# Last two attention units normalised on TensorE, a split out-projection, and new planner constants in a two-layer transformer kernel

## Chip, cores and metric

The kernel runs on one core of a Trainium2 chip. Its time is device microseconds of one execution; the median of three runs of the kernel before is 1628.04 us (1627.45 to 1629.54).

## What is computed

Two identical layers over 2048 rows of width 512. Each layer is an attention block and a gated feed-forward block, with the residual kept:

```python
x = x + _A_ref(_layernorm(x, axis=-1), A_wqkv, A_wo)               # 32 heads of width 16, softmax, out-projection
x = x + _B_ref(_layernorm(x, axis=-1), B_w_gate, B_w_up, B_w_down) # (gelu(x Wg) * (x Wu)) Wd, hidden width 1792
```

and both lines once more. In `_A_ref` the scores are q k^T / 4, the softmax runs over all 2048 keys, and each head's output is the softmax row times v. Inputs are bf16.

## The kernel before

The instruction order is not written by hand. A planner in `_emit_fast` runs at build time: it keeps a modelled clock for each engine, and at every step of its main loop it picks what TensorE does next, records it, and lets VectorE, GpSimd and SyncE take the jobs that have become ready ("pump", L490). Engines then run their recorded streams in order, with semaphore waits. So every constant of the planner moves instructions on all engines.

**Units.** Queries are cut into 4 blocks of 512 rows, heads into 8 groups of 4. A unit is one block and one group. Scores come out transposed (128 keys by 512 queries) in 64 tiles per unit: L1395, four heads side by side in the rows of the array. A tile is exponentiated either by ScalarE, two or three tiles in one ACTIVATE (L1409, written to fPT), or by VectorE, which makes the bits of an fp16 power of two (L1449, fPI) and three shifted copies (L1489, fPP). P times V (L1541) then accumulates in PSUM bank 7 with four heads in the columns of the array; a column of ones in V gives each head's row sum. In the last layer the last block is split in two halves of 256 queries, F0 and F1, 8 units each, so that F0's feed-forward can lie beside F1's attention.

**Closing a unit** (`evac` L936, `normalise` L863). VectorE copies bank 7 to fOS (L947). The row sums lie along one partition per head; a DMA turns them (fLT), VectorE inverts them (L871) and checks their bounds (L879), a DMA writes them to DRAM (rscr), the unnormalised heads go to DRAM too (oscr, four transfers), and for each pair of units two DMAs bring back the heads packed (fOP) and the inverse sums spread over partitions (fRB). GpSimd multiplies them into fAT (L912). Units are gathered in groups `sizes`: 6 and 2, and for F1 6, 1 and 1. The DMAs of F1's last unit are issued from ScalarE's queue (`move_act`), all others from SyncE's.

**After a block** (`post` L1042): out-projection (`mm_piece`, its matmuls at L643) plus residual (L1058), layer-norm statistics (L587, L588), scale on GpSimd (`ln_scale` L590: add of epsilon L595, power L597), application (L610), transposes (L616, or by DMA), gate (L1073, copied at L1092), Gelu (`gelus` L1353, which needs a table load on ScalarE and one back to Exp; for F1, L1095 applies Gelu to the gate's bank directly), up (L1073, multiplied at L1116), down (L1137), and the residual (L1159 or L1168). These are the "pieces" that the planner fits between the tiles of the next block.

**What sets the order.** `fill_ready` (L1314) gives the time F at which the next score tiles could start. P-times-V groups and pieces go in only if they end by then, or by the end of ScalarE's current work, plus a tolerance: 0.1 us for projections, 1.0 us for a `post` that is behind its pace, 99 us once it is behind by more than `LAG` = 24 us (`post_tol` L1659). `DVE_LATE` (L201) caps VectorE's backlog when it takes a tile. When nothing fits, and TensorE's modelled share of work in the last 3.4 us is under `DENSE` = 0.7, `keep_clock` (L1555) issues four matmuls on zeros, recorded at L1561.

Of the kernel before, what the change touches and what calls it, by code (L numbers as in the profile page):

```python
# [175 lines left out]
def _emit_fast(nc, es, x_in, wqkv, wo, wg, wu, wd, out, n_rep=2):  # L176
# [23 lines left out]
    NPART = 6  # L200
    DVE_LATE = 2.82  # L201
    WAIT_D = 0.45
# [37 lines left out]
    OS = sb("fOS", [128, NOS, 512], F32)  # L240
    LT = sb("fLT", [128, 128], F32)
    NRB = 1
    RB = sb("fRB", [128, NRB, 512], F32)
# [30 lines left out]
    def dma(eng, grp, dst, src, r=(), w=(), serial=False, kb=32):  # L274
        if grp not in sch.groups:
            sch.add_dma_group(grp, serial=serial)
        t = max(sch.free[eng], sch.ready(eng, r, w)) + 0.5
        wire[0] = max(t, wire[0]) + kb / 180.0
        return sch.op(eng, lambda e: e.dma_start(dst, src), r=r, w=w, grp=grp, cost=0.5, lat=wire[0] - t + 1.3)
# [198 lines left out]

    def move_act(prio, grp, dst, src, r, w, then, kb=32):

        then(dma("act", grp + "a", dst, src, r=r, w=w, serial=True, kb=kb))

    def starts_of(eng):
# [95 lines left out]

    def xn(i, alt):  # L580
        return HT[:, i + 4 * alt, 0:D].bitcast(F16)

    def xnkey(i, alt):
        return ("HT", i + 4 * alt)

    def stats(i, rows, key, then=None, prio=1):
        dve(prio, [(lambda e: e.bn_stats(ST[:, i, :], rows), [key], [("ST", i)], 0.72),  # L587
                   (lambda e: e.bn_aggr(MV[:, i, :], ST[:, i, :]), [("ST", i)], [("MV", i)], 0.1)], then)  # L588

    def ln_scale(n, then, lo=0, on="dve"):  # L590
        keys = [("MV", lo + i) for i in range(n)]
        mean = AP(MV, 2 * lo, [[16, 128], [2, n]])
        var = AP(MV, 2 * lo + 1, [[16, 128], [2, n]])
        job("pool", 1, [
            (lambda e: e.tensor_scalar(LNS[:, 0, lo:lo + n], var, LN_EPS, None, op0=ALU.add), keys,  # L595
             [("LNS", lo + i) for i in range(n)], 0.25),
            (lambda e: e.tensor_tensor(LNS[:, 1, lo:lo + n], LNS[:, 0, lo:lo + n], CM05[:, 0:n], op=ALU.pow),  # L597
             [("LNS", lo + i) for i in range(n)] + [("CM05",)], [("LNS", lo + i) for i in range(n)], 0.45 + 0.16 * n),
            (lambda e: e.tensor_scalar(LNS[:, 2, lo:lo + n], mean, -1.0, None, op0=ALU.mult),
             keys + [("LNS", lo + i) for i in range(n)], [("LNS", lo + i) for i in range(n)], 0.25)][:3 if on == "pool" else 2], then)  # L600

# [261 lines left out]
    def normalise(layer, qb, gs, half, h):  # L863
# [7 lines left out]
        ops = [(lambda e: e.reciprocal(LT[:, 0:nw], LT[:, 0:nw]), lk, lk, 0.07 + 0.0068 * nw)]  # L871
        final = h == 1 and gs[-1] == NG - 1
        go = move_act if final else move

        def then(o):
            there = []
            checks = []
            for lim, op in ((1.0 / L_LO, ALU.is_le), (1.0 / L_HI, ALU.is_ge)):
                checks.append((lambda e, lim=lim, op=op: e.scalar_tensor_tensor(  # L879
                    OKL[:, 0:nw], LT[:, 0:nw], lim, OKL[:, 0:nw], op0=op, op1=ALU.mult),  # L880
                    lk + [("OKL",)], [("OKL",)], 0.08 + 0.0018 * nw))
            dve(1, checks, got(("ok", layer, qb, h, gs[-1])))

            def stored(o, i):
                there.append(i)
                if len(there) == n:
                    lt["held"] = False
                    while lt["next"]:
                        lt["next"].pop(0)()
                g = gs[i]  # L890
                rs_here.add((layer, qb, h, g))
                if (layer, qb, h, g ^ 1) in rs_here:
                    pairs_q.append(((layer, qb * NG + (g | 1), h), lambda: spread(g & ~1)))
                    next_pair()

            for i in range(n):
                g = gs[i]
                go(0, "rs%d" % i, AP(RSC, (RC(qb, h, g) * 8 + g % 2) * 512, [[2 * 512, 4], [1, qn]]),
                   LT[:, w * i:w * i + w], [("LT", i)], [("RSC", RC(qb, h, g), g % 2)],
                   lambda o, i=i: stored(o, i), kb=8)  # L900

        def spread(g):
# [14 lines left out]
            def done(o):  # L917
# [6 lines left out]
                 [("OSD", d, j) for d in ds for j in range(4)], [("OP", slot)], landed, kb=qn / 2)  # L924
            go(0, "rb%d" % slot, RB[:, slot, 0:qn],
               AP(RSC, RC(qb, h, g) * 8 * 512, [[512, 8], [0, 16], [1, qn]]),
               [("RSC", RC(qb, h, g), k) for k in range(2)], [("RB", slot)], landed, kb=qn / 2)

# [7 lines left out]
    def evac(layer, u, part):  # L936
# [13 lines left out]
        def then(o):  # L950
# [3 lines left out]
            og = list(range(NG))  # L954
            sizes = [NG - 2, 1, 1] if h == 1 else [NG - 2, 2]
            pos = g
# [7 lines left out]
            bd = block_done[layer, qb, h] = block_done.get((layer, qb, h), 0) + 1  # L964

            gone = []

            def put(o):
                gone.append(o)
                if len(gone) == 4:  # L970
                    os_free.append(s)
                    stored_os.add((layer, u, h))
                    next_pair()
                    if h != 1 or g != NG - 1:
                        gathered(o)

            def put_out(o):
                for j in range(4):
                    move(0, "os%d_%d" % (s, j), OSD[d // 2, 32 * j + 16 * (d % 2):32 * j + 16 * (d % 2) + 16, 0:qn],
                         OS[32 * j:32 * j + 16, s, 0:qn], [("OS", s)], [("OSD", d, j)], put, kb=qn / 16)  # L980
                if h == 1 and g == NG - 1:
                    gathered(o)

# [8 lines left out]
            def gather():  # L992
                (move_act if h == 1 and g == NG - 1 else move)(0, "lt%d" % i, LT[:, w * i:w * i + w],
                     AP(OS, 16 * NOS * 512 + s * 512, [[32 * NOS * 512, 4], [1, qn]]),
                     [("OS", s)], [("LT", i)], put_out)
            if lt["held"]:
                lt["next"].append(gather)
            else:
                gather()
            if bd == NG:  # L1000
                posts.append(post(layer, qb, h))

        dve(0, [(fn, r, [("OS", s)], 0.086 + 0.001042 * qn)], then)

    def wchunk(s, jj, ck):
        return wslot(s)[:, ck * 256 + jj * 128:ck * 256 + (jj + 1) * 128]

    def ln_thread(tts, xsl, check, name, eng, step=2):

        nt = len(tts)  # L1010
        by_dma = step != 1

        def applied(i):
# [6 lines left out]
        def scale(lo):  # L1020
            hi = min(lo + step, nt)

            def apply(o):
                for i in range(lo, hi):
                    ln_apply(i, X[:, xsl[i], :], ("X", xsl[i]), eng, False, applied(i))
            ln_scale(hi - lo, apply, lo, eng)
            if check:
# [3 lines left out]
        for i, tt in enumerate(tts):  # L1031
# [5 lines left out]
            if not by_dma:  # L1037
                yield transpose_piece(i, tt, eng="act" if step == 1 and i % 2 == 0 else "dve", then=got(("tr", name, i)))
        while not all(("tr", name, i) in have for i in range(len(tts))):
            yield None  # L1040

    def post(layer, qb, h):  # L1042
# [10 lines left out]
        xload(n_)  # L1053
        while not all(("norm", layer, qb, h, g) in have for g in range(NG)) or n_ not in xhere:
            yield None
        for i, tt in enumerate(tts):
            def evac_x(b, i=i, x=xsl[i]):
# [5 lines left out]
                           + [("WO",)], evac_x, cols=D)  # L1063
        yield from ln_thread(tts, xsl, True, (layer, qb, 2, h), "dve" if qb == NQB - 1 else "pool",
                             1 if h == 1 else 2)
        xs = slice(512 * qb + q0, 512 * qb + q0 + qn)
# [162 lines left out]
    tiles_filled = [0]  # L1229
    LAG = 24  # L1230
    PRE = 1
# [110 lines left out]
    def fill():  # L1342
# [4 lines left out]
        if d is not None and not k_here(d):  # L1347
            d = None
        for x in a + ([d] if d is not None else []):
            cur.remove(x)  # L1350
# [295 lines left out]
    def behind():  # L1646
# [6 lines left out]
        elif NQB > 1 and posts_done[0] == total_posts - 2:  # L1653
            f = 0.5 * (at + 0.5 * NG - 1.0) / (0.5 * NG - 2.2)
        else:
# [3 lines left out]
    def post_tol():  # L1659
        if pace["haste"] or behind() > LAG:  # L1660
            return 99.0
        return 1.0 if behind() > 0 else 0.1

    sources = [Source(heads(), lambda: 0.1), Source(prep_source(), lambda: 0.1), Source(post_source(), post_tol)]
    DENSE = 0.7
    log = {"idle": 0.0, "warm": 0}

    while True:
# [10 lines left out]
        if posts_done[0] == total_posts and not any(jobs.values()):  # L1679
            break  # L1680
        if gelu_q and sch.ready("act", [("HT", i) for i in range(NFT)]) <= max(t, sch.free["act"]):
            gelus(*gelu_q.pop(0))
# [6 lines left out]
        if F is not None:  # L1689
            limit = max(F, sch.free["act"] - 0.437) - t  # L1690
        its = pv_ready(t)
        byj = [sum(1 for it in its if it[1] == j) for j in range(4)]
        fit = int((limit - change("col")) / MM + 0.29)
        full = min(byj)
# [7 lines left out]
        if press and its:  # L1702
            full = max(full, 1)
        want = 1 if pend.get(("PI", dg["n"] % NPI)) and not dg["items"] else 3
        if fit >= 1 and (full >= want or full and (rest or press)):
# [887 lines left out]
```

## Time and profile before

| | |
|---|---|
| median of three runs | 1628.04 us |
| the profiled execution's own time | 1627.3 us |
| its span | 1625.6 us |
| instructions | 38751 |
| TensorE / VectorE / ScalarE / GpSimd busy | 1546.1 / 1393.4 / 1542.8 / 175.6 us |
| Exp ACTIVATEs (L1409) | 1279: 638 of three tiles, 640 of two, 1 of one |
| tiles on VectorE (L1449) | 901 |
| matmuls of `keep_clock` (L1561) | 1692, busy 141.4 us |
| first exponential starts | 14.7 us |
| Gelu table loads and Gelus on ScalarE before the tail | 7 visits of 1.28 + 6.27 + 1.28 us, 1 of 1.28 + 3.29 + 1.28 us |

Times in views are microseconds from the start of the span. A line number is that of the kernel's source; many operations share the line of a helper. In the groups, the count behind "x" is followed by busy time, the mean of one in ns, and the engine's idle time just ahead of them with what ended it.

### The profile page before, as it was taken

What the parts mean: (1) busy time and instruction counts of PE and PEld (TensorE: products, weight loads), DVE (VectorE), ACT (ScalarE), POOL (GpSimd) and SP (SyncE); (2) the same over time, 40 slices, a digit from 0 to 9 for tenths busy, and PEclk for the clock granted to TensorE, in tenths of its full rate; (3) what the DMA queues carried; (4) which work ended last, traced back from release to release, by engine and by line L of the source; (5) the groups of instructions that cost most, each with busy time, mean ns of one, the idle gap of its engine ahead of it and who ended that gap; (6) DMA issues with size and microseconds to landing.
All of it is one profiled execution on the core that took longest, in us unless ns stands there. A gap on an engine that the chain in (4) does not pass through costs nothing.

```text
span 1625.6 us, 38751 instructions
## 1 busy us (share of the span) xinstructions
PE 1546.1 (95%) x16400; PEld 509.6 (31%) x16400; DVE 1393.4 (86%) x2403; ACT 1542.8 (95%) x1323; POOL 175.6 (11%) x219
## 2 busy tenths in 40 slices
PE   8999999999999999999999999999999999999998
PEld 3333222222222222322332322222222222444454
DVE  7999998889988899987743999988899889898793
ACT  6999999999999999999999999999999999999991
POOL 2321010002100111002410100100110000100000
PEclk9999999999999999999999999999999999999999
DMA  5200111125111421114223111221411114113244
GB/s 149 60 8 6 47 35 53 44 63 123 28 49 47 116 60 34 41 56 109 60 73 111 38 45 34 66 56 31 129 28 43 53 27 123 37 47 88 75 112 134
DMA packets 162370, 103.26 MB, mean 64 GB/s; under 512 B 54928, under 2 KB 145296, under 8 KB 162192
## 3 DMA queue, kind: packets, MB, share of 16 engines
q1 hardware_dynamic: 158096, 95.98, 22.4%
q0 software_dynamic: 2112, 4.19, 1.0%
q8 instruction: 133, 2.18, 0.6%
q10 hardware_dynamic: 1984, 0.53, 0.1%
q14 instruction: 45, 0.37, 0.1%
HBM read 76.81 MB, written 15.20 MB: 57 GB/s over the span
## 4 chain that ended last, share of the span: by engine, by line
PE 42%; ACT 34%; DVE 18%; DMA 3%; issue 1%; POOL 1%; SPq 0%; DVEq 0%; POOLq 0%; ACTq 0%
ACT fPT L1409 32%; PE fPS L1541 12%; PE fPS L1395 12%; PE fPS L1073 9%; DVE fPI L1449 8%; DVE fPP L1489 6%; PE fPS L1137 4%; PE fPS L643 3%; ACT fHT L1358 2%; DMA fRB<-rscr 2%; PE fPS L1561 1%; DMA rscr<-fLT 1%; DVE fQ L689 1%; DVE fHT L1092 1%; DVE fOS L947 1%
## 5 line engine op out<-in xcount | busy, mean ns | idle before, releaser
L1409 ACT ACTIVATE fPT<-fPS 128x1536 bf16<-128x1536 f32 x1279 | 1466.9, 1263 | 38.8 <-PE fPS L1395 33.3
L1449 DVE TENSOR_SCALAR fPI<-fPS 128x512 int16<-128x512 f32 x901 | 610.1, 685 | 72.1 <-PE fPS L1395 67.5
L1395 PE MATMUL fPS<-fQ,fKT 32*128 32x512 f16 (+1 forms) x4608 | 514.9, 360 | 42.4 <-ACT fPT L1409 27.4
L1489 DVE TENSOR_SCALAR fPP<-fPI 128x2048 int16<-128x2048 int16 (+3 forms) x747 | 467.7, 649 | 10.0 <-PE fPS L1541 6.3
L1541 PE MATMUL fPS<-fPT,fVP 128*17 128x512 bf16 (+1 forms) x3591 | 462.9, 359 | 6.0 <-DVE fOS L947 3.0
L1541 PE MATMUL fPS<-fPP,fVD 128*17 128x512 f16 (+1 forms) x3051 | 426.0, 357 | 4.8 <-DVE fPP L1489 2.6
L1395 PEld LDWEIGHTS fPS<-fQ,fKT 32*128 32x128 f16 x4608 | 139.2, 91 | 514.9 <-ACT fPT L1409 356.9
L1541 PE MATMUL fPS<-fPI,fVP 128*17 128x512 f16 (+1 forms) x1017 | 268.4, 359 | 2.8 <-DVE fOS L947 1.4
L1073 PE MATMUL fPS<-fXNT,fWR 128*128 128x512 f16 (+1 forms) x952 | 219.7, 362 | 8.9 <-DVE fHT L1116 4.2
L1541 PEld LDWEIGHTS fPS<-fPT,fVP 128*17 128x17 f16 x3591 | 117.5, 88 | 149.8 <-issue 89.7
L912 POOL TENSOR_TENSOR fAT<-fOP,fRB 128x512 f16<-128x512 f32 (+1 forms) x36 | 43.8, 1216 | 1055.1 <-DMA fRB<-rscr 1027.6
L1541 PEld LDWEIGHTS fPS<-fPP,fVD 128*17 128x17 f16 x3051 | 114.8, 89 | 118.6 <-issue 51.0
L1561 PE MATMUL fPS<-fONB,fZV 128*17 128x512 f16 x1692 | 141.4, 390 | 1.7 <-POOL fQMASK L372 1.5
L1137 PE MATMUL fPS<-fWR,fHT 128*128 128x512 bf16 x428 | 118.4, 383 | 0.4 <-DVE fPI L1449 0.3
L1073 PEld LDWEIGHTS fPS<-fXNT,fWR 128*128 128x128 bf16 x952 | 76.8, 97 | 116.3 <-DVE fPI L1449 27.1
L1116 DVE TENSOR_TENSOR fHT<-fPS,fHT 128x512 bf16<-128x512 f32 x112 | 76.3, 689 | 41.2 <-PE fPS L1073 29.7
L1092 DVE CAST fHT<-fPS 128x512 bf16<-128x512 f32 x105 | 71.5, 687 | 29.8 <-PE fPS L1073 29.7
L1541 PEld LDWEIGHTS fPS<-fPI,fVP 128*17 128x17 f16 x1017 | 68.3, 89 | 42.9 <-issue 18.1
L723 POOL TENSOR_SCALAR fVD<-fVP 128x544 f16<-128x544 f16 (+1 forms) x48 | 56.6, 1178 | 128.6 <-DVE fVP L731 125.9
L947 DVE COPY fOS<-fPS 128x512 f32<-128x512 f32 (+1 forms) x72 | 45.0, 625 | 14.3 <-PE fPS L1541 13.6
L1561 PEld LDWEIGHTS fPS<-fONB,fZV 128*17 128x17 f16 x1692 | 39.3, 91 | 42.6 <-issue 25.1
L689 DVE TENSOR_SCALAR fQ<-fPS,fQMASK 128x512 f16<-128x512 f32 (+1 forms) x72 | 46.1, 683 | 2.9 <-PE fPS L643 2.9
(69 smaller groups left out, 595.0 us busy)
## 6 DMA issues: line engine op xcount, KB each, us to landing
fWR<-in_B_w_up_dram SPq DMA_DIRECT2D x62, 256.0 KB, 2.9
fWR<-in_B_w_down_dram SPq DMA_DIRECT2D x58, 256.0 KB, 2.7
fWR<-in_B_w_gate_dram SPq DMA_DIRECT2D x57, 256.0 KB, 4.5
oscr<-fOS SPq DMA_DIRECT2D x224, 32.0 KB, 1.7
fOP<-oscr SPq DMA_DIRECT2D x28, 256.0 KB, 2.7
fRB<-rscr SPq DMA_DIRECT2D x28, 256.0 KB
fX<-in_A_x_dram POOLq DMA_DIRECT2D x4, 1024.0 KB, 5.7
xscr<-fX SPq DMA_DIRECT2D x16, 256.0 KB, 3.1
```

Of the source, the lines that this page charges most:

```text
L689: ops.append((lambda e, p=p, slot=slot: e.tensor_scalar(Q[:, slot, q0:q0 + qn], bank(b)[:, 0:qn], QMASK[:, p:p + 1], None, op0=ALU.mult), ...
L947: fn = lambda e: e.tensor_copy(OS[:, s, 0:qn], bank(ACC)[:, 0:qn])
L1073: ins = e.matmul(bank(bs[0])[:, w * qn:(w + 1) * qn], lhsT=wchunk(s, (ft + w) % 2, ck), rhs=XNT[:, ck, xs], start=(ck == 0), stop=(ck == N ...
L1092: evac_job(1, b, [(lambda e: e.tensor_copy(in_ht(ft), in_bank(b)), [BK[b]], fk, 0.6)], got(("gate", layer, qb, h, ft)))
L1116: (lambda e: e.tensor_tensor(in_ht(ft), in_bank(b), in_ht(ft), op=ALU.mult), [BK[b]] + fk, fk, 0.62)], got(("up", layer, qb, h, ft))))
L1137: ins = e.matmul(bank(b)[:, 0:D], lhsT=HT[:, ft, i * 128:(i + 1) * 128], rhs=wslot(s)[:, jj * D:(jj + 1) * D], start=(ft == 0), stop=(ft = ...
L1395: ins = e.matmul(bank(b)[:, b0:b0 + qn], lhsT=KT[32 * j:32 * j + 32, (x[1] % NG) // 2, kt * 128:(kt + 1) * 128], rhs=Q[32 * j:32 * j + 32, ...
L1409: o = sch.op("act", lambda e: e.activation(PT[:, p, 0:512 * na].rearrange("p (a b) -> p a b", a=na), PS[:, b0:b0 + na, :], ACTF.Exp, scale ...
L1449: dve(0, [(lambda e: e.tensor_scalar(PI[:, gi, 512 * r:512 * (r + 1)], bank(bd), DBIAS, 0.0, op0=ALU.add, op1=ALU.max), [BK[bd]], [("PI", ...
L1489: shifts.append((s, [(lambda e: e.tensor_scalar(PP[:, s, 0:512 * n], PI[:, gi, 0:512 * n], int(OCT) * ph // NPH, None, op0=ALU.add), [("PI ...
L1541: ins = e.matmul(PS[32 * j:32 * j + VW, ACC, 0:qn], lhsT=l, rhs=r_, start=a, stop=z, tile_position=(0, 32 * j), skip_group_check=True)
L1561: ins = e.matmul(PS[32 * j:32 * j + VW, ACC, :], lhsT=ZV[:, :], rhs=ones, start=False, stop=False, tile_position=(0, 32 * j), skip_group_c ...
```

## The change

- The last two units of F1 (groups 6 and 7) no longer take the way through DRAM. `direct` turns the row sums with two fp32 matmuls, VectorE inverts them from PSUM, eight fp32 matmuls against an identity spread them over 32 partitions per head, and VectorE multiplies fOS by them, with a mask that zeroes all but the 16 rows of each head. Group 6 lands in fAT's last chunk, group 7 in a tile of its own (fATL). `move_act` is gone; `sizes` is 6 and 2.
- F1's out-projection becomes `lead`: for each of its two row tiles four matmuls (fAT, with group 6 in the last chunk) that leave the bank open, and, when group 7 is there, one matmul with fATL against fWOS, a copy of the last 128 rows of wo rotated by 16, so that they meet the rows that group 7 fills. Two DMAs load fWOS early; GpSimd makes the fp32 identity (fIDF) and the mask (fHEADS) in the head.
- In F1's layer norm epsilon is added by VectorE right behind the statistics, and the normalised rows go to fPT's storage instead of fHT's.
- When no score tile is left, ScalarE gets a one-column Gelu, so that the table is loaded there.
- Planner constants: `DVE_LATE` 2.82 to 2.87, the modelled DMA rate 180 to 280, `LAG` 24 to 38.7, `DENSE` 0.7 to 0.58, the tolerances 1.0 to 0.89 and (projections) 0.1 to 0.02, the least P-times-V group 3 to 4 matmul rounds, the fit margin 0.29 to 0.3, ScalarE's lead 0.437 to 0.44, F1's pace 2.2 to 1.8.

```diff
-    DVE_LATE = 2.82
+    DVE_LATE = 2.87
...
-        wire[0] = max(t, wire[0]) + kb / 180.0
+        wire[0] = max(t, wire[0]) + kb / 280.0
...
-            sizes = [NG - 2, 1, 1] if h == 1 else [NG - 2, 2]
+            sizes = [NG - 2, 2]
...
+            if h == 1 and g >= NG - 2:
+                os_of.pop((layer, u, h))
+                directs.append(direct(g, s))
+                return
...
+    def direct(g, s):
+        lo = 8 * (g - NG + 2)
+        def turn_sums(e, bs):
+            for c in range(2):
+                ins = e.matmul(bank(bs[0])[:, 4 * c:4 * c + 4], lhsT=OS[:, s, 128 * c:128 * c + 128],
+                               rhs=AP(IDF, 16, [[128, 128], [32, 4]]), start=True, stop=True)
+            return ins
...
+            evac_job(0, b, [(lambda e: e.reciprocal(LTL[:, lo:lo + 8], bank(b)[:, 0:8]), [BK[b]], [("LTL", g)], 0.17)], inverted)
...
+        def spread_sums(e, bs):
+            for c in range(2):
+                for j in range(4):
+                    ins = e.matmul(bank(bs[0])[32 * j:32 * j + 32, 128 * c:128 * c + 128],
+                                   lhsT=AP(LTL, lo + 4 * c + j, [[16, 128], [0, 32]]), rhs=IDF[:, :],
+                                   start=True, stop=True, tile_position=(0, 32 * j), skip_group_check=True)
+            return ins
...
+                ops = [(lambda e, c=c, dst=dst: e.scalar_tensor_tensor(
+                    dst, OS[:, s, 128 * c:128 * c + 128], HEADS[:, 0:1], bank(b)[:, 128 * c:128 * c + 128],
+                    op0=ALU.mult, op1=ALU.mult), [BK[b], ("OS", s), ("HEADS",)], w, 0.22)]
...
+    def lead(layer, qb, h):
...
+                for c in range(NCK):
+                    ins = e.matmul(bank(bs[0])[:, 0:D], lhsT=AT[:, c, cols], rhs=WO[:, c, :], start=(c == 0), stop=False)
...
+            yield Piece(MM, [("ATL", NG - 1, i), ("WOS", 0), ("WOS", 112)], lambda e, bs, i=i: e.matmul(
+                bank(bs[0])[:, 0:D], lhsT=ATL[:, 128 * i:128 * i + 128], rhs=WOS[:, :], start=False, stop=True),
+                evac_x, held=boxes[i])
+        yield from ln_thread(tts, xsl, True, name, "dve", 1)
...
-    LAG = 24
+    LAG = 38.7
...
-            f = 0.5 * (at + 0.5 * NG - 1.0) / (0.5 * NG - 2.2)
+            f = 0.5 * (at + 0.5 * NG - 1.0) / (0.5 * NG - 1.8)
...
-        return 1.0 if behind() > 0 else 0.1
+        return 0.89 if behind() > 0 else 0.1
...
-    sources = [Source(heads(), lambda: 0.1), Source(prep_source(), lambda: 0.1), Source(post_source(), post_tol)]
-    DENSE = 0.7
+    sources = [Source(queue_source(directs), lambda: 1.0), Source(queue_source(leads), lambda: 1.0), Source(heads(), lambda: 0.1), Source(prep_source(), lambda: 0.02), Source(post_source(), post_tol)]
+    DENSE = 0.58
...
+        if not left() and not table["gelu"]:
+            sch.op("act", lambda e: e.activation(ACTD[:], CM05[:, 0:1], ACTF.Gelu_apprx_tanh), r=[("CM05",)], w=[("ACTD",)],
+                   cost=1.5)
+            table["gelu"] = True
...
-            limit = max(F, sch.free["act"] - 0.437) - t
+            limit = max(F, sch.free["act"] - 0.44) - t
...
-        fit = int((limit - change("col")) / MM + 0.29)
+        fit = int((limit - change("col")) / MM + 0.3)
...
-        want = 1 if pend.get(("PI", dg["n"] % NPI)) and not dg["items"] else 3
+        want = 1 if pend.get(("PI", dg["n"] % NPI)) and not dg["items"] else 4
```

## The prediction

> **What bounds the kernel now.** First the page's busy times and its 40 slices, which say where the bound is; then the groups with shapes kept apart, for prices; then ScalarE's waits by hundreds of microseconds; then the chain that ended last, for the tail; last, windows of 3.41 us around the one place where the granted clock falls.
>
> ```profile
> PE 1546.1 (95%) x16400; PEld 509.6 (31%) x16400; DVE 1393.4 (86%) x2403; ACT 1542.8 (95%) x1323; POOL 175.6 (11%) x219
> ...
> ACT  6999999999999999999999999999999999999991
> ```
>
> ScalarE (ACT) is full in every slice but the first and the last. TensorE (PE) is as busy, but part of that is filling:
>
> ```profile
> L1409 ACT ACTIVATE fPT<-fPS 128x1536 bf16<-128x1536 f32 x638 | 941.9, 1476 | 32.1 <-PE fPS L1395 28.2
> L1409 ACT ACTIVATE fPT<-fPS 128x1024 bf16<-128x1024 f32 x640 | 673.3, 1052 | 6.7 <-PE fPS L1395 5.1
> L1561 PE MATMUL fPS<-fONB,fZV 128*17 128x512 f16 x1692 | 141.4, 390 | 1.7 <-POOL fQMASK L372 1.5
> ```
>
> The exponentials set the pace and stand still for 33.3 us in all, waiting for score tiles (L1395); by its waits, 6.8 us of that lie in the first 100 us, so 26.5 us between 100 and the tail. TensorE's 1692 matmuls on zeros are 141.4 us of its time. So until about 1584 us the time is ScalarE's work plus those waits; behind that, a chain:
>
> ```profile
> 1585.37 0.44 DVE fOS L947
> 1585.83 2.11 DMA fLT<-fOS
> 1587.96 0.21 DVE fLT L871
> 1588.20 1.96 DMA rscr<-fLT
> ...
> 1590.23 3.84 DMA fRB<-rscr
> ...
> 1594.20 0.73 POOL fAT L912
> ...
> 1594.98 1.05 PE fPS L643 x4
> 1596.06 0.70 DVE fX L1058
> ...
> 1602.59 11.47 PE fPS L1073 x104
> ```
>
> Start and duration of each step: three DMAs (7.91 us) between the last unit's copy and its out-projection, then 6.5 us of layer norm, then 104 feed-forward matmuls without a gap.
>
> **The change, part by part.** The sum is made against the profiled execution, 1627.3 us (span 1625.6), 0.7 under the median of 1628.04.
>
> *Tail, last unit to first residual.* Before: last P-times-V ends at 1585.33, the residual add L1058 starts at 1596.06: 10.7 us. After, by the recorded order of the changed program, TensorE runs 2 down matmuls, 4 out-projection, 2 turning, 4 out-projection, 8 spreading, 4 down, 2 closing ones. A 512-column matmul in a stream takes 0.216 (four L1073 halves and L643 x4 agree: 1.05 for four with 0.17 of latency). So 6 x 0.216 = 1.3 us until turning; the copy to fOS (0.42) is over by then. Turning and spreading are fp32 and have no row here. Nearest rows: L1201, a lone matmul of 2 columns, 0.16, and the LDWEIGHTS of 128 columns, 0.09. [...] I take 0.7 and 0.7. The inverse (0.20) lies under the 4 out-projection matmuls (0.86). Then two multiplications on VectorE: L947 took 0.684 at 512 and 0.419 at 256 columns, so about 0.29 at 128; 0.6 and a handover. They lie beside 4 down matmuls (0.86). Then 0.22 and 0.17. Sum 1.3 + 0.7 + 0.86 + 0.7 + 0.86 + 0.39 = 4.8 us: 5.9 saved (6.7 at the cheapest fp32, 4.7 at the dearest).
>
> *What becomes late next.* F0's 28 down matmuls lay in the DMA waits (1585.26 to 1592.6) for nothing. Now 6 lie ahead of the closing matmuls and 22 behind them, 22 x 0.227 (16 took 3.63) = 5.0 us ahead of the transposes on TensorE. The layer norm by rows: two adds 1.36, statistics and aggregation twice 1.7, two epsilon adds 0.2, one F0 residual (L1159, 0.69) recorded in between, a bound check 0.15, two applications 1.0: the second tile is there at 5.0 too. Transposes, the second F0 residual ahead of the last copy, and that copy: 1.2. So 6.2 after 6.5: 0.3 saved. The power on GpSimd (0.57) hides; its two adds of epsilon (0.23 and 0.42) go. F1's feed-forward weights are freed later, by k: the first 2.2 us behind the closing matmuls and used 9 us later; seven loads of 256 KB took about 0.7 us each to issue, so they still arrive.
>
> *Gelu table.* L1095's load took 1.28 us at 1603.65 while TensorE ran on (the 104 matmuls): its removal is worth nothing. The new load stands behind the last exponential, where ScalarE is idle until 1600: nothing; without that cover 1.28.
>
> *Group 6.* About 1.4 us of fp32 and nothing less on TensorE just ahead of F0's Gelu, where both engines are full; VectorE's five operations replace three. Half on the path: +0.7 (0 to +1.6). The queues lose 11 transfers on SyncE and 3 on ScalarE; the two weight loads for fWOS are recorded behind the first seven gate loads, ahead of the first turning of sums at 24 us: nothing.
>
> *Head.* GpSimd makes fIDF and fHEADS ahead of the first scale (about 0.4); VectorE waits for the statistics of rows 2 and 3 until 7.7 anyway: nothing. But the modelled DMA rate now puts the first statistics of block 1 ahead of the second pair's application. That transfer was issued at 2.7 and took 6.1: 8.8. So 8.8 + 0.69 + 0.18 against 9.13: the pair is 0.6 late, and so is the first exponential. +0.6 (0 to +1.3).
>
> *Exponentials.* The order holds 639 two-tile ACTIVATEs for 640 and 903 tiles on VectorE for 901: -1.05. VectorE's shifts come to +3 us in 1393, with 230 idle: nothing.
>
> *Constants, 100 to 1580 us.* The order holds 784 zero matmuls for 1692: 227 groups of 0.33 = 76 us of TensorE less, and 73 changes between kinds fewer. Most of that was idle time, so it isn't a gain in itself. The gain can only be in ScalarE's 26.5 us of waits: pieces may overrun the next tile by 0.11 (projections 0.08) less, and are forced in only when 38.7 us behind. Some 40 of the 79 waits, 0.2 to 0.6 each near the ends of feed-forward blocks, shrink by about 0.1: -3.5, and the clock's fall below, -1.5, if it doesn't come back. -5 (from -13, half of the waits gone, to +4, backlog pushed into later tiles).
>
> Sum: -5.9 - 0.3 + 0.7 + 0.6 - 1.05 - 5 = -10.9: 1616.4 on the profiled execution, 1617.1 beside the median.
>
> [...] Columns: stretch, length, then busy us of TensorE, its weight loads, VectorE, ScalarE, GpSimd, then granted clock.
>
> ```profile
> 1403.29:1406.70 3.41, 2.52 (x53) 1.19 (x56) 3.30 (x6) 3.41 (x4) 0.00 (x0) 0.96 0.24 49
> 1406.70:1410.12 3.42, 3.42 (x38) 1.12 (x29) 2.26 (x6) 2.62 (x3) 2.69 (x5) 0.50 0.06 15
> 1410.12:1413.53 3.41, 3.41 (x49) 1.13 (x52) 2.17 (x4) 2.65 (x3) 0.00 (x0) 0.54 0.40 82
> ```
>
> After a stretch busy 2.52 of 3.41 us, and no zero matmul in it, the clock was halved for 6.8 us, and ScalarE lost 0.80 + 0.76 us, some 1.5. [...] The row decides: I count one such fall removed and one or none new.
>
> **Rivals.**
> - *Waits stay* (0.20): ScalarE's waits follow from the tiles' own order and not from crowding; only the tail and the rest count: -5.9, or -2 with slow fp32 and a late chunk of fAT (its third chunk came at 1581, 4 us early). 1622 to 1626, likeliest 1622. For it: TensorE was never the bound on average. Against: every wait's releaser is L1395.
> - *Half of the waits go* (0.13): TensorE's real load was 1405 us of 1626, with zeros in the way at each tile; -13 in place of -5: 1609.
> - *Slower: the clock falls often* (0.04). Between 100 and 1580, wherever zero matmuls went. -10.9 is used up at 7 falls of 1.5 us; from 10 on it is slower by over 0.2%; 12 give 1635. For: the row above; against: the guard is thinned, not removed, and 1 fall in 1480 us.
> - *Doesn't do what it says* (0.03): group 7's path still waits for something on a queue (a chunk of fAT late): the tail keeps 10 us: 1623.
>
> **How the numbers follow.** The likeliest case (0.60) is 1617.1, itself from 1612 to 1622. Range 1609 to 1625: it takes in half of the waits on one side and the unchanged waits on the other, and leaves out the clock and the worst tail. About 0.2% (3.3 us) is what a measurement here can tell from no change: faster means below 1624.8: 0.60 + 0.13 + 0.16 + 0.02 = 0.91; within 0.2%: 0.05; slower 0.04.
>
> **What would show it.** Right: the first residual of F1 starts some 5 us after the last unit's copy, no DMA stands between; the transposes follow F0's last down matmuls with no gap; ScalarE's waits sum to 25 to 30 us in all; the table load falls behind the last exponential and the feed-forward stretch is no shorter. Wrong: the last copy to fOS not some 5 us earlier than 1585 (the constants gave nothing), turning or spreading over 1 us, the granted clock under 1.0 in several stretches, or a DMA ahead of the out-projection.

## The result, and the profile after

After takes 1616.13 us (median of 4 runs, 1614.04 to 1616.86), before in the same comparison 1628.79 (4 runs, 1627.45 to 1630.70): the ratio is 0.9919, interval 0.9902 to 0.9937. Beside the experiments below before ran another 85 times, in batches of 21, 14 and 50 with medians of 1627.94, 1627.80 and 1627.85 us. After's profiled execution is the slowest of its four: 1616.86 us, with a span of 1615.1; before's span was 1625.6. So 10.5 us of the profiled span went, where the medians lie 12.7 apart.

The page's line of busy times, and ScalarE's line of its 40 slices:

```profile
PE 1483.8 (92%) x15466; PEld 493.4 (31%) x15528; DVE 1393.7 (86%) x2420; ACT 1539.8 (95%) x1323; POOL 175.3 (11%) x218
...
ACT  6999999999999999999999999999999999999992
```

ScalarE still fills every slice but the first and the last. TensorE is 62 us less busy, and that is no gain in itself. The groups of after, shapes kept apart (busy, mean ns | idle just ahead and what ended it; lines are numbered some hundred higher than before, L1395 is now L1492, L1409 is L1506, L1561 is L1658):

```profile
L1506 ACT ACTIVATE fPT<-fPS 128x1536 bf16<-128x1536 f32 x638 | 948.1, 1486 | 34.4 <-PE fPS L1492 30.3
L1506 ACT ACTIVATE fPT<-fPS 128x1024 bf16<-128x1024 f32 x639 | 679.5, 1063 | 3.1 <-PE fPS L1492 2.5
L1658 PE MATMUL fPS<-fONB,fZV 128*17 128x512 f16 x784 | 65.4, 394 | 1.5 <-POOL fQMASK L378 1.5
```

The matmuls on zeros are the 784 of the recorded order. The exponentials still wait 32.8 us for scores (30.3 + 2.5), where before they waited 33.3: the waits as a sum have hardly moved. The chain of the tail has changed (start, duration, engine and tile):

```profile
1581.67 0.86 PE fPS L1081 x4
1582.53 0.34 PE fPS L1021 x4
1582.87 0.88 PE fPS L1081 x4
1583.75 0.57 PE fPS L1041 x16
1584.33 0.97 PE fPS L1232 x4
1585.30 0.43 PE fPS L1092 x2
1585.73 3.02 PE fPS L1232 x14
...
1592.11 11.53 PE fPS L1168 x104
```

Ahead of these lines the last P-times-V ends (it starts at 1579.93 and takes 1.20 us). From there to the feed-forward matmuls (L1168) no DMA stands in the chain any more. Turning (L1021) and spreading (L1041) lie between the halves of the out-projection (L1081), its closing matmuls (L1092) follow F0's down matmuls (L1232), and the first residual add starts at 1585.55. The table load of the new Gelu starts at 1580.22, directly behind the last exponential.

Cut at four marks, the two profiled spans compare so:

| stretch, us | before | after | difference |
|---|---|---|---|
| start to the last copy to fOS | 1585.37 | 1581.18 | -4.2 |
| that copy to F1's first residual add | 10.69 | 4.37 | -6.3 |
| residual add to first feed-forward matmul | 6.46 | 6.56 | +0.1 |
| feed-forward to the end | 23.08 | 22.99 | -0.1 |

The first 4.2 us are, by ScalarE: first exponential at 17.25 for 14.66 (+2.6); idle time from there to the last exponential 31.9 for 35.1 (-3.2); exponentials 1463.4 busy for 1466.9 (-3.5). The sum is -4.2 (rounded). Of the idle time, -1.3 lies between 20 and 100 us; between 100 and 1540 us the waits for scores make -2.0 (25.7 to 23.7) and gaps too short to be put down to anything -0.6; behind 1540 us it grew by 0.6.

### The profile page after: what moved, and what is told of

Read it like the earlier page. It is cut to its first block, busy times and chain, and to the rows that moved or that the text cites. A ratio compares the mean times of both kernels' runs of the same rounds, so it can differ in the third digit from the quotient of the medians.

```text
span 1615.1 us, 36926 instructions
## 1 busy us (share of the span) xinstructions
PE 1483.8 (92%) x15466; PEld 493.4 (31%) x15528; DVE 1393.7 (86%) x2420; ACT 1539.8 (95%) x1323; POOL 175.3 (11%) x218
## 3 DMA queue, kind: packets, MB, share of 16 engines
q1 hardware_dynamic: 157592, 95.84, 22.5%
## 4 chain that ended last, share of the span: by engine, by line
ACT 44%; PE 35%; DVE 15%; DMA 3%; POOL 1%; issue 1%; SPq 1%; DVEq 0%; POOLq 0%
ACT fPT L1506 41%; PE fPS L1638 10%; PE fPS L1492 10%; PE fPS L1168 8%; DVE fPI L1546 6%; DVE fPP L1586 5%; PE fPS L1232 4%; PE fPS L651 3%; ACT fHT L1455 2%; DMA fRB<-rscr 1%; DMA fXNT<-fHT 1%; DVE fHT L1187 1%; ACT L1455 1%; POOL fAT L917 0%; DVE fOS L952 0%
## 5 line engine op out<-in xcount | busy, mean ns | idle before, releaser
L1506 ACT ACTIVATE fPT<-fPS 128x1536 bf16<-128x1536 f32 x1278 | 1463.4, 1274 | 37.6 <-PE fPS L1492 32.8
L1492 PE MATMUL fPS<-fQ,fKT 32*128 32x512 f16 (+1 forms) x4608 | 509.3, 359 | 70.7 <-ACT fPT L1506 49.0
L1638 PE MATMUL fPS<-fPT,fVP 128*17 128x512 bf16 (+1 forms) x3593 | 454.0, 359 | 13.8 <-DVE fOS L952 5.0
L1638 PE MATMUL fPS<-fPP,fVD 128*17 128x512 f16 (+1 forms) x3045 | 419.1, 358 | 5.2 <-DVE fPP L1586 3.3
L1492 PEld LDWEIGHTS fPS<-fQ,fKT 32*128 32x128 f16 x4608 | 137.2, 91 | 532.9 <-ACT fPT L1506 381.3
L1638 PE MATMUL fPS<-fPI,fVP 128*17 128x512 f16 (+1 forms) x1015 | 268.8, 359 | 3.6 <-DVE fOS L952 1.7
L1168 PE MATMUL fPS<-fXNT,fWR 128*128 128x512 f16 (+1 forms) x952 | 219.9, 362 | 12.1 <-DVE fHT L1211 6.4
L1638 PEld LDWEIGHTS fPS<-fPT,fVP 128*17 128x17 f16 x3593 | 116.8, 88 | 158.1 <-issue 91.6
L1638 PEld LDWEIGHTS fPS<-fPP,fVD 128*17 128x17 f16 x3045 | 112.7, 89 | 117.1 <-issue 51.3
L1232 PE MATMUL fPS<-fWR,fHT 128*128 128x512 bf16 x383 | 108.7, 382 | 7.9 <-issue 4.8
L1168 PEld LDWEIGHTS fPS<-fXNT,fWR 128*128 128x128 bf16 x952 | 76.9, 98 | 118.7 <-DVE fPI L1546 28.4
L1638 PEld LDWEIGHTS fPS<-fPI,fVP 128*17 128x17 f16 x1015 | 67.2, 88 | 42.8 <-issue 17.2
L1658 PE MATMUL fPS<-fONB,fZV 128*17 128x512 f16 x784 | 65.4, 394 | 1.5 <-POOL fQMASK L378 1.5
L952 DVE COPY fOS<-fPS 128x512 f32<-128x512 f32 (+1 forms) x72 | 44.9, 624 | 11.5 <-PE fPS L1638 10.5
L1455 ACT ACTIVATE fHT<-fHT 128x3584 bf16<-128x3584 bf16 (+1 forms) x16 | 47.2, 2995 | 0.1
```

The source lines that it names most:

```text
L1168: ins = e.matmul(bank(bs[0])[:, w * qn:(w + 1) * qn], lhsT=wchunk(s, (ft + w) % 2, ck), rhs=XNT[:, ck, xs], start=(ck == 0), stop=(ck == N ...
L1232: ins = e.matmul(bank(b)[:, 0:D], lhsT=HT[:, ft, i * 128:(i + 1) * 128], rhs=wslot(s)[:, jj * D:(jj + 1) * D], start=(ft == 0), stop=(ft = ...
L1455: sch.op("act", lambda e, lo=lo, hi=hi: e.activation(HT[:, lo:hi, q0:q0 + qn], HT[:, lo:hi, q0:q0 + qn], ACTF.Gelu_apprx_tanh), r=keys, w= ...
L1492: ins = e.matmul(bank(b)[:, b0:b0 + qn], lhsT=KT[32 * j:32 * j + 32, (x[1] % NG) // 2, kt * 128:(kt + 1) * 128], rhs=Q[32 * j:32 * j + 32, ...
L1506: o = sch.op("act", lambda e: e.activation(PT[:, p, 0:512 * na].rearrange("p (a b) -> p a b", a=na), PS[:, b0:b0 + na, :], ACTF.Exp, scale ...
L1638: ins = e.matmul(PS[32 * j:32 * j + VW, ACC, 0:qn], lhsT=l, rhs=r_, start=a, stop=z, tile_position=(0, 32 * j), skip_group_check=True)
```

## Theories and experiments

My theory is the prediction's sum, called *the sum* below: structure (tail, about -6) and constants (about -5) add up, and the constants work by making other work overrun the score tiles less. The rival is the *drawn order*: the planner draws a new order for every set of constants; this set fits this program, and has no gain of its own. (The letters in the expectations stand for what each of them says.)

The order of a program can be read without running it, and that already speaks against the sum: with all else new, setting `LAG` back to 24, or F1's pace back to 2.2, or the tolerance back to 1.0, leaves the order of every engine unchanged, instruction for instruction, and so do the three together. My -3.5 us rested on two of these three, and on the projections' tolerance. `DVE_LATE` (2.82), the modelled DMA rate (180), the projections' tolerance (0.1), `DENSE` (0.7), ScalarE's lead (0.437) and the least P-times-V group (3) each reorder thousands of lines.

All twelve runs, with before and after. Each ratio is to before in the run's own batch. "Waits" is ScalarE's idle time ahead of exponentials, between 100 and 1540 us; "half clock" is the time at a granted clock of 0.5 in the profile's clock record, which starts 5 to 7 us into the span (14.3 in dense_head, whose head it doesn't cover). The half-clock stretch that each record breaks off in, around the kernel's end, is left out. dense_07's output is wrong (a relative error of 0.30; why, is not known), so its time is weak evidence:

| run | us | ratio to before, interval | span | waits | half clock |
|---|---|---|---|---|---|
| before | 1627.85 | 1 | 1625.6 | 25.7 | 6.8 |
| after | 1616.13 | 0.9919, 0.9902 to 0.9937 | 1615.1 | 23.7 | 10.2 |
| structure_only | 1634.90 | 1.0044, 1.0031 to 1.0058 | 1634.7 | 30.1 | 6.8 |
| constants_only | 1643.72 | 1.0083, 1.0063 to 1.0102 | 1642.4 | 39.2 | 27.3 |
| lead_joined | 1615.03 | 0.9925, 0.9908 to 0.9942 | 1613.0 | 22.5 | 6.8 |
| no_gelu_early | 1615.27 | 0.9935, 0.9918 to 0.9952 | 1610.0 | 20.0 | 6.8 |
| dense_none | 1641.31 | 1.0082, 1.0059 to 1.0105 | 1641.1 | 38.5 | 92.2 |
| dense_07 (wrong output) | 1623.60 | 0.9970, 0.9959 to 0.9981 | 1621.5 | 27.7 | 6.8 |
| dense_head | 1613.55 | 0.9911, 0.9898 to 0.9924 | 1611.5 | 20.6 | 3.4 |
| want_3 | 1623.98 | 0.9981, 0.9969 to 0.9994 | 1620.0 | 25.3 | 6.8 |
| head_rate | 1614.91 | 0.9923, 0.9906 to 0.9940 | 1613.5 | 22.4 | 6.8 |
| head_both | 1622.83 | 0.9966, 0.9955 to 0.9976 | 1625.0 | 33.9 | 23.9 |
| before_late | 1629.83 | 1.0015, 1.0007 to 1.0023 | 1627.3 | 26.7 | 3.4 |
| before_want4 | 1627.60 | 0.9992, 0.9979 to 1.0006 | 1627.2 | 27.0 | 6.8 |

**The two halves.** structure_only is after with all ten constants at their old values:

```diff
-    DVE_LATE = 2.87
+    DVE_LATE = 2.82
-    LAG = 38.7
+    LAG = 24
-    DENSE = 0.58
+    DENSE = 0.7
...
```

> The changed kernel with all ten planner constants put back to their old values; row sums by TensorE, split out-projection and early Gelu table stay. Theory (structure and constants are two separate gains): the stretch from the last copy to fOS to the first feed-forward matmul falls from 17.1 us to about 10.9 as in the changed kernel, the last copy stays near 1585 us: 6.2 less than before, 1622.5 us. Rival (the short tail needs the new constants, since F0's down matmuls have to be left over to cover the layer norm): less than 4 us gained, 1625 or more. Rival (the constants gave nothing, their 4 us came from the structure): 1618 or less.

constants_only is before with all ten new values, and the guard for an empty list that a least group of four needs:

```diff
-    DVE_LATE = 2.82
+    DVE_LATE = 2.87
...
+        if not a:
+            a, d = [d], None
```

> The kernel before with the new planner constants alone (and the guard for an empty tile list that they need). Theory: the last copy to fOS comes some 4 us earlier, the tail stays as it was: 1624.5 us. It should hold a half-rate stretch of the clock in the first 20 us, as the changed kernel does. Rival (the 4 us came from the structure): 1628 to 1629.

Both are slower than before, by 7.0 and 15.9 us, while both together are 11.7 faster (all against 1627.85). The sum fails in both. In structure_only the tail itself does what was predicted: from the last copy to the feed-forward matmuls it takes 10.6 us, for before's 17.15 and after's 10.93. But that copy comes at 1597.44, 12.1 us later than before, and F1's down matmuls have holes. Groups of structure_only, then TensorE's timeline near its end:

```profile
L1506 ACT ACTIVATE fPT<-fPS 128x1536 bf16<-128x1536 f32 x639 | 945.4, 1480 | 36.8 <-PE fPS L1492 32.0
L1506 ACT ACTIVATE fPT<-fPS 128x1024 bf16<-128x1024 f32 x641 | 676.6, 1056 | 10.6 <-PE fPS L1492 10.0
```

```profile
1620.84 2.12 PE L1658 MATMUL fPS<-fONB,fZV 128*17 128x512 f16 x36
...
1624.73 1.69 PE L1658 MATMUL fPS<-fONB,fZV 128*17 128x512 f16 x28
```

The waits for scores are 42.0 us in all (8.7 more than before, by the last figures of the two rows), ScalarE has four more tiles than before, and 64 zero matmuls fill the time in which F1's down matmuls wait: 26.6 us from the first feed-forward matmul to the end, for 23.1. In constants_only the last copy comes at 1593.15, 7.8 us later than before, and gate and up projections of F0 slipped past the last exponential. Its chain:

```profile
1591.92 1.19 PE fPS L1543 x34
1593.12 6.22 PE fPS L1073 x56
```

After the last P-times-V (L1543) come 56 matmuls of F0's gate and up projections (L1073), its Gelu's table load starts at 1594.76 behind 4.0 us of idle ScalarE, and its down matmuls stand ahead of the out-projection, so that copy to residual takes 19.6 us and not 10.7. Part of its loss is the clock: it spent 27.3 us at half clock, for before's 6.8. At mean clocks of 0.996 and 0.995 it ran in 1637.2 and 1638.5 us, where before ran in 1630.3 and 1633.4 (means of five and four runs). So at an equal clock it loses 5 to 7 us; structure_only, at 1.000, loses 6.9 (1632.7, four runs, for 1625.8).

**Parts of the new tail.** lead_joined waits for group 7 ahead of the whole out-projection, so that its eight matmuls and the two closing ones come in a row; no_gelu_early leaves the dummy Gelu out (every other engine's order is after's):

```diff
-        while not all(("norm", layer, qb, h, g) in have for g in range(NG - 1)):
+        while not all(("norm", layer, qb, h, g) in have for g in range(NG)):
```

```diff
-        if not left() and not table["gelu"]:
-            sch.op("act", lambda e: e.activation(ACTD[:], CM05[:, 0:1], ACTF.Gelu_apprx_tanh), r=[("CM05",)], w=[("ACTD",)],
-                   cost=1.5)
-            table["gelu"] = True
```

> The changed kernel with F1's out-projection started only when group 7 is there too: the order differs in the tail alone; the same four-matmul halves, issued behind the spreading. Theory A (the split itself matters: the residual waits for nine matmuls more): from the last copy to the first residual 5.2 to 5.6 us in place of 4.4, and as much more at the first feed-forward matmul, about +1 us. Theory B (TensorE has the same down and out-projection matmuls to do either way and the transposes follow them without a gap): the residual is later but the first feed-forward matmul is not, within 0.3 us.

> The changed kernel without the one-column Gelu behind the last exponential: all other engines' streams are identical, and ScalarE loads the Gelu table at F1's first gate. Theory (the load lies beside the 104 feed-forward matmuls either way): the last stretch from the first feed-forward matmul to the end stays at 23.0 us and the time at the changed kernel's 1616, within 0.7. Rival (the load is on the path): 1.3 us more in that stretch.

lead_joined's chain:

```profile
1579.80 0.34 PE fPS L1021 x4
1580.14 0.45 PE fPS L1232 x2
1580.59 0.57 PE fPS L1041 x16
1581.16 0.54 PE fPS L1232 x2
1581.70 1.73 PE fPS L1081 x8
1583.43 0.43 PE fPS L1092 x2
1583.86 2.59 PE fPS L1232 x12
```

The residual add comes 0.4 us later after the copy (4.80 for 4.37), and the feed-forward matmuls not at all: 10.93 us behind the copy in both. The down matmuls of F0 that remain, here 19 and in after 21, fill TensorE ahead of the transposes either way. So opening the out-projection early is worth nothing at the end of this program; the tail's gain lies in the rest of the new path, which has no DMA left. Without the early table load, the load falls at 1586.21 beside the feed-forward matmuls, and they take 23.03 us to the end for 22.99: nothing, as predicted. The two medians lie 1.1 (lead_joined) and 0.9 us under after's, inside the range of its four runs.

**Zero matmuls and the clock.** dense_none lets them in only in the plan's first 25 us (52 of them), dense_07 goes back to the old share (1520), dense_head to the old share in the first 25 us only:

```diff
-        if acc["free"] and not over[0] and density(t) < DENSE and (F is None or F - t >= change("col") + MM) \
+        if acc["free"] and not over[0] and density(t) < (0.7 if t < 25.0 else 0.0) and (F is None or F - t >= change("col") + MM) \
```

```diff
-    DENSE = 0.58
+    DENSE = 0.7
```

```diff
-        if acc["free"] and not over[0] and density(t) < DENSE and (F is None or F - t >= change("col") + MM) \
+        if acc["free"] and not over[0] and density(t) < (0.7 if t < 25.0 else DENSE) and (F is None or F - t >= change("col") + MM) \
```

> The changed kernel without any zero matmuls after the first 25 us (52 in place of 784; the tiles' order changes with it). Theory (a stretch that is three quarters busy lets the clock fall, each fall costs ScalarE 1.5 to 1.8 us): several half-rate stretches between 100 and 1580 us, four or more, and 1622 us or more. Rival (TensorE's real work keeps the clock up): none or one of them, 1613 to 1617.

> The changed kernel with DENSE = 0.7 everywhere: 1520 zero matmuls instead of 784, at the price of another order of the tiles. Theory (zero matmuls cost nothing by themselves, the guard keeps the clock up): no half-rate stretch in the head, time 1614 to 1616 us. Rival (zeros in TensorE's stream hold tiles back, so that thinning them is the gain of the constants): ScalarE's waits grow by 4 us or more and the time is 1619 to 1621.

> The changed kernel with DENSE = 0.7 for the first 25 us of the plan and 0.58 after; the only difference in any engine's stream is one more group of four zero matmuls between the first transposes. Theory (the head's half-rate clock costs what the first exponential is late by): no half-rate stretch between 10 and 17 us, first exponential 2 us earlier, at about 14.8 instead of 17, and the whole 2 us less: 1614 us. Rival (other engines make up for a late head within the first 100 us): the first exponential is earlier and the time is within 0.5 us of the changed kernel's.

With so few zeros the clock is halved in 16 places, 92.2 us in all, and the time is 25.2 us above after's. Part of that is another order: F0's Gelu slipped behind the last exponential here too, and from the last copy to the run of 104 feed-forward matmuls it takes 21.8 us for 10.9. So the clock's own share is not separated; but the zeros are not shown to be wasted: after, with 784 of them, has two falls and 10.2 us at half clock. More zeros did not help: dense_07 is 7.5 us slower than after, with another order (and a wrong output), and the fall that it has lies in the head, where its expectation had none. dense_head differs from after in one group of four zeros in the head, and that did not mend the head: K's four matmuls took 1.86 us and the first exponential came at 16.70, not at 14.8. Its 1613.55 and after's 1616.13 have overlapping intervals.

**Neighbours of both programs.** If the new values were better rules, a step back from after should lose about what the same step forward gains in before.

```diff
-        want = 1 if pend.get(("PI", dg["n"] % NPI)) and not dg["items"] else 4
+        want = 1 if pend.get(("PI", dg["n"] % NPI)) and not dg["items"] else 3
```

> The changed kernel with one planner constant put back: the least P-times-V group 3 rounds in place of 4. Theory (the constants are worth something only as a set that was fitted to this very program, and any other order lands elsewhere): 1622 to 1640 us, with more waits of ScalarE or a late Gelu of F0. Rival (each constant brings its own few tenths): within 2 us of the changed kernel's 1616.

before_want4 is the reverse step in before (with the guard for an empty list), before_late is before with `DVE_LATE = 2.87` alone:

> Before, with a least group of four P-times-V matmuls instead of three (and the guard for an empty list that this needs), nothing else. After loses 7.9 us when it goes back from four to three. If four is the better rule in itself (theory A): before gains some 4 to 8 us by it, 1620 to 1624. If the set is fitted to the program (theory B): before loses, 1630 to 1643.

> Before, with the modelled lateness of VectorE at 2.87 instead of 2.82 and nothing else; thousands of lines of TensorE's order shift. If the new constants hold better values (theory A): 1628 or a little less. If each set of constants is only fitted to its own program (theory B): slower than before by 2 to 15 us, with more of ScalarE's waits for scores between 100 and 1540 us than before's 25.7.

want_3 loses 7.9 us against after; before_want4 gains nothing that can be told (-0.25, interval across 1), and before_late loses 2.0. So four is not the better rule in itself, and that goes against the sum. But neither is before so finely fitted that each step costs much, as the drawn order had it (2 to 15 us in both): the one step cost the least that it allowed, the other nothing. before_late reached its last copy at 1578.91, 6.5 us earlier than before, because F0's Gelu and its table load slipped behind the last exponential, and paid it back: copy to residual 18.7 us.

**The head.** after's first exponential came 2.6 us late. head_rate models the old DMA rate in the plan's first 8 us, which restores VectorE's old order there and changes no order behind some 220 us; head_both adds the old share of zeros in the first 25 us, and that redraws the order behind:

```diff
-        wire[0] = max(t, wire[0]) + kb / 280.0
+        wire[0] = max(t, wire[0]) + kb / (180.0 if t < 8.0 else 280.0)
```

> After, with the modelled DMA rate at 180 as before for transfers issued in the plan's first 8 us and at 280 behind them. Streams differ from after's in the head and up to some 150 us (VectorE's first applications stand ahead of the second block's statistics again), not behind. If the head's 2.6 us are due to VectorE's order (theory A): first exponential back at 14.7 to 15.2, last copy to fOS 2 us earlier than after's 1581.2, 1614. If they are due to the clock's fall in the head (theory B, the head's zero matmuls are as thin as after's): first exponential at 16.5 to 17.2, time as after, 1616.

> head_rate, with the zero matmuls of the plan's first 25 us at the old share (0.7) too; this gives another order from 150 us on (thousands of lines). If heads and orders add (theory A): first exponential at 14.6, and 1612 or less. If the order behind the head decides (theory B): the first exponential at 14.6 as well, but the time anywhere between after's 1616 and the 1624 of the runs with other orders, since the waits for scores are drawn anew.

head_rate's first exponential came at 16.55: the value that its expectation gives for the clock, not for VectorE's order. The same matmuls of the head in before and then in head_rate:

```profile
11.43 1.02 PE L643 MATMUL fPS<-fXNT,fWK 128*128 128x512 f16 x4 [0.78 <-ACT fXNT L625]
12.29 1.03 PE L643 MATMUL fPS<-fXNT,fWQ 128*128 128x512 f16 x4
```

```profile
11.70 1.86 PE L651 MATMUL fPS<-fXNT,fWK 128*128 128x512 f16 x4 [0.56 <-ACT fXNT L633]
13.36 1.91 PE L651 MATMUL fPS<-fXNT,fWQ 128*128 128x512 f16 x4
```

With K and Q at half speed the Q copies, which the first scores wait for, start 1.9 us later (15.31 for 13.43). after has the same two groups at 1.86 and 1.91. It is 0.7 us later still (17.25 for 16.55): its V matmuls, which its scores stand behind, took 1.67 us for 1.11 as the half clock went on, and K starts 0.15 later (11.85 for 11.70). That 0.15 is not the price of VectorE's order, since head_rate's half clock began earlier (8.34 for 9.66) and slowed its transposes ahead of K. VectorE's own rows show the price, first in before, then in after:

```profile
9.13 0.74 DVE L610 TENSOR_SCALAR fHT<-fX,fMV,fLNS 128x512 f16<-128x512 bf16 x2 [0.61 <-POOL fLNS L597]
```

```profile
8.76 0.69 DVE L593 BATCH_NORM_STATS2 fST<-fX 128x6 f32<-128x512 bf16 x1 [0.76 <-DMA fX<-in_A_x_dram]
9.49 0.18 DVE L594 BATCH_NORM_AGGREGATE fMV<-fST 128x2 f32<-128x6 f32 x1
9.59 0.70 DVE L618 TENSOR_SCALAR fHT<-fX,fMV,fLNS 128x512 f16<-128x512 bf16 x2
```

The second pair's application starts 0.46 us later, behind the statistics of block 1, and K's matmuls 0.42 later (11.85 for 11.43). So some 0.4 of the 2.6 us are VectorE's order and some 2.1 the clock.

Whether the thinner zeros made the head's clock fall is not settled. The records show 6.8 us at half clock in the head with the new share (10.2 in constants_only), and with the old share 3.4 in four runs, but 6.8 in dense_07 and dense_none, which keep the new DMA rate. With the old zeros and the old rate (head_both) Q takes 1.27 us and the first exponential comes at 15.78. before itself isn't always spared: in the profiles of before_late and before_want4, whose heads are before's, it came at 15.21 and 15.30. For the whole time all that weighs little. head_rate's 1614.91 lies within the range of after's runs, and part of a late head comes back: ScalarE's waits from 20 to 100 us are 1.5 us in every run with the new DMA rate and 2.5 to 3.0 in those with the old one in the head.

head_both is 6.7 us slower than after. There the clock can be separated from the order, since each execution has its mean granted clock: its 21 runs go from 1617.8 and 1618.4 us at 0.998 to 1626.8, 1627.1 and 1627.1 at 0.993. At 0.998 the others stand at 1614.0 and 1616.7 (after), 1614.5 and 1615.3 (head_rate), 1621.7 to 1623.0 (want_3), 1623.3 and 1623.6 (dense_07), 1636.4 (structure_only), and before at 1628.4 (mean of six runs). So about 3 us of head_both's loss are its order (from two runs on each side), and the rest is that this order makes the clock fall more often.

## Why the prediction was right, and where it was not

1616.13 us against 1617.1, and 1616.86 against 1616.4 on the profiled execution: the sum held. Its tail held by the mechanism that was named. Its other part, from the start to the last copy, came out at -4.2 us for -4.75 (group 6, head, exponentials and constants) because misses cancel, and that is luck: the exponentials gave 2.5 us more than counted and group 6 cost 0.7 less, while the head cost 2.0 more and ScalarE's idle time gave 3.2 where 5 were counted.

- *Tail, -5.9*: right; -6.3 by copy to residual. No run shows the 0.7 and 0.7 that I took for turning and spreading, nor the cheapest and the dearest fp32 beside them: they were my estimates, and in the chain the two took 0.34 and 0.57. Each of the 2 and 8 fp32 matmuls stands as two MATMULs (x4, x16), and a 128-column one takes 0.273 us, as long as a 16-bit one of 256 columns (0.274, L1638). Much of this lies beside other work: turning's weight loads (0.63 us in all, from 1582.15) for the most part beside the out-projection's matmuls, and spreading's sixteen records of 0.273 us fit into 0.57.
- *Residual to feed-forward, 6.2*: it is 6.56. F0's down matmuls were through 4.9 us after the residual add (counted: 5.0); the transposes, F0's second residual add and the last copy behind them took 1.65 and not 1.2.
- *Table load 0*: right, by no_gelu_early.
- *Group 6, +0.7*: nothing is left over for it in the balance of ScalarE, which closes to about a tenth.
- *Head, +0.6*: wrong in size, +2.6. The step that it counted, VectorE's order, is there and costs about 0.4. The rest is TensorE at half clock from about 9.7 to 16.5 us: the prediction put nothing down for the clock in the head, and before's profile was one in which it held.
- *Exponentials, -1.05*: -3.5. One two-tile ACTIVATE fewer is in it, as counted. For the other 2.5 us the rows show that ACTIVATEs overlap more: their durations sum to 1627.6 us in after and 1615.2 in before (the two shapes), while the time they cover went down. That they overlap more because fewer of them wait (65 waits for 76 between 100 and 1540 us) is argued, not shown; constants_only, with 84 waits, covers 1463.6 us too.
- *Constants, -5*: the step failed. ScalarE's waits from 100 us to the tail were to shrink by 3.5 us; they went from 26.5 to 25.3. In all they are 32.8 and not the 25 to 30 that the prediction named as its sign. The step said "pieces may overrun the next tile by 0.11 (projections 0.08) less, and are forced in only when 38.7 us behind". The 0.11 and the 38.7 by themselves move no instruction, and the ten constants together, put into before, cost 15.9 us (5 to 7 at an equal clock). So they showed no gain of their own; what there is belongs to this pair of program and order.
- *The clock's fall, -1.5*: it did come back, at another place (217.88 us). Columns as in the prediction, after:

```profile
215.00:218.43 3.43, 1.91 (x20) 0.70 (x22) 3.06 (x5) 3.43 (x4) 1.27 (x1) 0.92 0.03 8
218.43:221.84 3.41, 3.41 (x24) 0.72 (x22) 2.71 (x5) 1.59 (x2) 0.00 (x0) 0.58 0.00 0
```

At first there is a stretch in which TensorE was busy for 1.91 of 3.43 us and waited 1.01 us for GpSimd with an out-projection at the head of its queue; then half clock, and ScalarE 1.8 us without work. no_gelu_early has the same order on TensorE and no fall there, and its span is 5.1 us shorter; how much of that is this fall the two profiles don't say.

The rival "waits stay" (1622) describes after's neighbours better than after. want_3, dense_07 and head_both, each one constant or two away, gave 1622.8 to 1624.0 with the new tail in full (10.6 us from copy to feed-forward in each). want_3 is the clean case: at an equal clock of 0.998 it stands 6.7 us above after. dense_07's output is wrong, and more than half of head_both's loss is the clock. Two more, head_rate and dense_head, gave what after gives. So the new tail with another of these orders gains some 4 us (with the old constants it loses 7); the further 7 or 8 us come with some orders only. Which lines of an order make the waits is not settled by these runs. No version here is measurably better than after; dense_head's median is lowest, with overlapping intervals.

The rival "the clock falls often" priced a fall too low: it took 1.5 us for the 6.8 us at half clock in before's profile, and 50 runs of before say 1.5 us for every 3.4 (below). It didn't decide after, but it has a part in dense_none and constants_only, and more than half of head_both's loss.

## What to carry to other kernels

The chain of three DMAs (7.91 us) between the last tile and the projection that depends on it cost most of its length here, where no other work was left to cover it: 6.3 us of 10.7 went with it, and TensorE did the turning and the spreading in 0.9 us, fp32 included. Look then at what else fills TensorE, since it, and not the new chain, may set the next step. Where a planner writes the order, test a change of structure and a change of its constants apart and with neighbours: here each half alone lost and both together won, so a set of constants that was good in one program was not good in the other. Compare runs at an equal granted clock before calling a difference of a few microseconds an effect of the order: in 50 runs of before, five thousandths of mean clock went with 7.6 us.

## What the runs showed of the hardware

The 39 half-clock stretches in the 14 clock records of this case are 3.41, 6.83 or 10.24 us long (the one at the end of each record, which breaks off, left out). They began where TensorE's work was thin: in the 3.41 us ahead of each of the 39, TensorE was busy for 0.9 to 2.7 us and no gap within them was longer than 2.6 us; ahead of after's fall at 217.88 it was busy for 2.2 us and the longest gap was 0.7. With the same stream on TensorE the clock fell there in one execution (after, 3.41 us) and not in another (no_gelu_early). What a fall cost can be read from the 50 runs of before's last batch, by their mean clock over the program: 1625.8 us at 1.000 (12 runs), 1627.6 at 0.999 (20), 1628.4 at 0.998 (6), 1629.4 at 0.997 (3), 1630.3 at 0.996 (5), 1633.4 at 0.995 (4). From 1.000 to 0.995 are five thousandths, each 3.3 us at half clock (0.001 x 1626 / 0.5), and 7.6 us of time: 1.5 us per step, about half of the time at half clock. In these 50 runs the mean clock goes with two thirds of the variance of the time. The price was not the same for every order: per thousandth of mean clock it was 0.9 us in want_3 (1622.1 at 0.998 to 1629.5 at 0.990) and 1.8 in head_both (1618.1 at 0.998 to 1627.0 at 0.993).
